# Attention followed by soft MoE: q loaded one quad earlier, the first quads reordered, the MoE mask moved, three expert weights issued later, and three small edits in the tail

One core of a Trainium2 chip. The metric is the time of one execution on the device, in microseconds; every run is checked against the reference.

## The reference

```python
# q, k, v: (8, 12, 448, 64) float32; phi: (768, 32); w1: (8, 768, 1024); w2: (8, 1024, 768)
q_n, k_n = rmsnorm(q, g_q), rmsnorm(k, g_k)              # over head_dim
attn = softmax(q_n @ k_n.T / 8);  o = attn @ v            # per batch and head
x = o.transpose(0, 2, 1, 3).reshape(3584, 768)
logits = x @ phi                                          # 32 slots, 4 for each of 8 experts
d = softmax(logits, axis=0);  slot_input = d.T @ x
for e in range(8):
    slot_out[e] = relu(slot_input[e] @ w1[e]) @ w2[e]
c = softmax(logits, axis=1);  out = c @ slot_out          # (3584, 768) float32
```

## The kernel before

A quad is four heads of one batch: 24 quads, 3 to a batch. The loop is software-pipelined by hand. In round Q the scores and exponentials of quad Q run, beside the normalisation and transposes of later quads and the output of quad Q - 1; every third round the MoE logits and slot sums of a batch fall in. q, k and v go over the SP queue (448 KB each for a quad); 16 expert weights of 3.1 MB (float32) go over the GpSimd queue, cast to bf16 on the way. The slots meet the experts only when the last batch has been summed, then the output is formed and stored.

```python
place("rawq", 2 * 2 * NT * D, 4)     # four buffers of raw q
place("rawk", 2 * 2 * NT * D, 3)
place("qkn", 2 * NT * 128, 1)        # one buffer of scaled q and one of scaled k
place("vraw", 2 * 2 * NT * D, 2)
...
load(0, 0); load(0, 1)               # (quad, 0 = q / 1 = k), cut: g_q, g_k
load(1, 0); load(1, 1); loadv(0); load(2, 0); load(2, 1); loadv(1)
...
square(1, 1); rowsum(1, 1); rsqrt(2, 1, 2); scaleqk(1, 1); vcopy(0)   # end of the prologue
WQ = [0, 2, 4, 6, 9, 11, 13, 16, 18, 20, 21, 21, 22, NQ, NQ]          # round of each weight's issue
for Q in range(NQ + 2):
    for q4 in (3, 4) if Q == 0 else (Q + 4,):
        if q4 < NQ:
            load(q4, 0); load(q4, 1)
    score(Q, 0)
    if Q + 3 < NQ and Q:
        square(Q + 3, 0)             # ScalarE: the q that was issued in round Q - 1
    if ahead and Q:
        square(Q + 2, 1, True)       # GpSimd: k
    # cut: transposes and evictions of Q + 1, scaleqk(Q + 2, 0), scores 1 to 3, outputs
    if mb is not None:
        moe_logits(mb)               # ends with Exp on ScalarE, then memset(e[0:64, 3], 0) on VectorE
    norm(Q - 1, 1, 1); rowsum(Q + 2, 1)
    # cut: loadv(Q + 3); moe_x; rsqrt(Q + 3); scaleqk(Q + 2, 1)
    moe_evac(Q - 1)
    if mb is not None:
        moe_sin(mb)                  # slot-input matmuls read e
    # cut: scores 5 and 6; loadw(i) where WQ[i] == Q
```

The softmax here doesn't subtract the row's maximum and nothing guards it: scores larger than these inputs give would overflow.

## Time and profile before

| | before |
|---|---|
| median of 3 runs | 293.72 us (290.98 to 295.19) |
| span of the profiled run, clock granted to TensorE | 289.4 us, 0.861 |
| attention ends (last output matmul group starts) | 215.3 us |
| TensorE begins the last group of the expert layers | 252.3 us |
| first output matmul / first output issued | 255.9 / 258.5 us |
| ScalarE's waits for q | 8.2 us, 8 times |

ScalarE squares one q per round, so the starts of these squares date the rounds, and their distances are the length of a round. The profiled run is one of the faster ones of this kernel; about half of its later runs took 292 to 294 us.

### The profile page before, as it was taken

The page shows a single profiled execution, that of the slowest core. Times are in us where ns is not written, and L with a number is a line of the kernel's source. Part 1 is how long each engine was busy: PE and PEld are TensorE (multiplying, and loading weights), DVE is VectorE, ACT ScalarE, POOL GpSimd, SP SyncE. Part 2 cuts the span into 40 slices and gives each one's busy share as a digit, 9 for nine tenths or more (in the row PEclk, how much of TensorE's full clock was granted, in tenths as well). Part 3 has the DMA queues.
Part 4 walks back from the last instruction along what each step waited for, and adds up shares of the span by engine and source line. Part 5 has one row for each costly group of instructions (what it writes and reads, how often), then busy time and mean ns, then how long its engine had stood idle before and what let it go on. Part 6 is the DMA issues. An engine that isn't in the chain of part 4 may idle for free.

```text
span 289.4 us, 8498 instructions
## 1 busy us (share of the span) xinstructions
PE 222.8 (77%) x3564; PEld 159.6 (55%) x3564; DVE 193.3 (67%) x411; ACT 190.5 (66%) x272; POOL 164.1 (57%) x187
## 2 busy tenths in 40 slices
PE   7748888888788888898886889988887764789800
PEld 2326565666565666667654666756666764743300
DVE  5837888798768979888885988887553100158700
ACT  4496999789679988997977899788770000037600
POOL 0466999698867888897884988879302000000000
PEclk9958999999999999999999999999996555555555
DMA  6998999999999899999999999969999999519995
GB/s 187 263 286 218 209 264 246 265 283 228 283 247 271 211 213 241 268 240 279 255 267 260 226 240 243 235 158 195 186 207 211 211 214 210 103 68 408 409 413 228
DMA packets 44918, 69.81 MB, mean 241 GB/s; under 512 B 3920, under 2 KB 36688, under 8 KB 44880
## 3 DMA queue, kind: packets, MB, share of 16 engines
q1 hardware_dynamic: 29184, 44.05, 51.4%
q0 software_dynamic: 15376, 25.22, 48.3%
q8 instruction: 28, 0.46, 0.6%
q14 instruction: 10, 0.08, 0.1%
q10 hardware_dynamic: 320, 0.00, 0.1%
HBM read 83.46 MB, written 11.01 MB: 326 GB/s over the span
## 4 chain that ended last, share of the span: by engine, by line
PE 29%; DVE 20%; DMA 17%; ACT 15%; issue 7%; POOL 6%; SPq 1%; ACTq 0%; POOLq 0%; DVEq 0%
DMA arena<-in_q_dram 14%; ACT arena L246 10%; DVE ss L189 7%; PE sc L245 5%; POOL arena L201 5%; DVE arena L230 5%; PE hTp L461 4%; DVE arena L268 4%; PE soTp L470 4%; PE op L500 4%; PE qkTp L219 3%; PE ov L258 3%; ACT arena L181 2%; DMA arena<-in_k_dram 2%; PE op L501 2%
## 5 line engine op out<-in xcount | busy, mean ns | idle before, releaser
L246 ACT ACTIVATE arena<-sc 128x896 bf16<-128x896 f32 x168 | 143.0, 919 | 7.5 <-PE sc L245 7.4
L245 PE MATMUL sc<-arena 128*128 128x448 bf16 x336 | 92.6, 358 | 21.5 <-ACT arena L246 19.2
L201 POOL TENSOR_TENSOR arena<-arena,rs 128x896 bf16<-128x896 f32 x47 | 80.5, 1714 | 41.0 <-ACT rs L194 35.8
L258 PEld LDWEIGHTS <-arena 128*128 128x128 bf16 x1344 | 57.5, 98 | 18.0 <-issue 0.8
L258 PE MATMUL ov<-arena 128*128 128x65 bf16 (+1 forms) x1344 | 62.9, 198 | 0.2 <-ACT arena L246 0.2
L189 DVE TENSOR_REDUCE ss<-arena 128x14 f32<-128x896 f32 x48 | 51.7, 1077 | 6.1 <-ACT arena L181 6.1
L245 PEld LDWEIGHTS <-arena 128*128 128x128 bf16 x336 | 26.8, 98 | 33.1 <-issue 28.7
L268 DVE TENSOR_TENSOR arena<-ov,rd 128x256 bf16<-128x256 f32 x96 | 40.7, 424 | 3.3
L504 ACT ACTIVATE wown<-op,arena 128x768 f32<-128x768 f32 x14 | 12.4, 900 | 42.3 <-PE op L501 42.3
L179 POOL TENSOR_TENSOR arena<-arena 128x896 f32<-128x896 f32 x21 | 35.4, 1686 | 0.2
L181 ACT ACTIVATE arena<-arena 128x896 f32<-128x896 f32 x27 | 25.6, 950 | 9.8 <-DMA arena<-in_q_dram 8.2
L230 DVE COPY arena<-qkTp 64x896 bf16<-64x896 bf16 x48 | 29.8, 620 | 2.0 <-PE qkTp L219 0.9
L219 PE MATMUL qkTp<-ident,arena 128*128 128x128 bf16 x360 | 27.7, 223 | 2.5 <-DVE arena L226 0.8
L219 PEld LDWEIGHTS <-arena 128*128 128x128 bf16 x360 | 22.9, 100 | 10.1 <-POOL arena L201 5.0
L279 PE MATMUL xTp<-ident,arena 128*128 128x128 bf16 x192 | 18.1, 220 | 11.0 <-DVE arena L268 11.0
L267 DVE RECIPROCAL rd<-ov 128x4 f32<-128x4 f32 x96 | 17.0, 177 | 12.6 <-PE sc L245 6.7
L226 DVE TENSOR_SCALAR arena<-qkTp,gg 128x896 bf16<-128x896 bf16 x24 | 16.4, 684 | 11.8 <-PE qkTp L219 11.0
L279 PEld LDWEIGHTS <-arena 128*128 128x128 bf16 x192 | 12.6, 97 | 18.9 <-DVE arena L268 14.4
L193 ACT ACTIVATE ss<-ss,eps 128x28 f32<-128x28 f32 (+1 forms) x27 | 8.5, 315 | 17.2 <-DVE ss L189 17.2
L282 DVE COPY arena<-xTp 128x1024 bf16<-128x1024 bf16 x24 | 16.4, 683 | 2.1 <-PE xTp L279 2.1
L506 DVE TENSOR_SCALAR wown<-op,arena 128x768 f32<-128x768 f32 x14 | 14.2, 1017 | 4.6 <-PE op L501 4.4
L500 PE MATMUL op<-arena,eT 32*128 32x512 bf16 x28 | 16.0, 616 | 1.4 <-ACT wown L504 0.7
(62 smaller groups left out, 192.7 us busy)
## 6 DMA issues: line engine op xcount, KB each, us to landing
wown<-in_moe_w_dram POOLq DMA_DIRECT2D x11, 1536.0 KB, 15.6
arena<-in_q_dram SPq DMA_DIRECT2D x24, 448.0 KB, 7.6
arena<-in_k_dram SPq DMA_DIRECT2D x24, 448.0 KB, 8.9
out_dram<-wown SPq DMA_DIRECT2D x12, 768.0 KB, 9.0
arena<-in_moe_w_dram POOLq DMA_DIRECT2D x5, 1536.0 KB, 21.3
arena<-in_v_dram SPq DMA_DIRECT2D x48, 128.0 KB, 6.8
arena<-in_v_dram SPq DMA_DIRECT2D x48, 96.0 KB, 7.2
out_dram<-wown SPq DMA_DIRECT2D x4, 384.0 KB, 9.1
```

Of the source, the lines that this page charges most:

```text
L179: nc.gpsimd.tensor_tensor(sq(t), r, r, op=MUL)
L181: nc.scalar.activation(out=sq(t), in_=r, func=ACTF.Square)
L189: nc.vector.reduce_sum(sss[n][:, t], sq(t).rearrange("p (r d) -> p r d", d=D), axis=AX)
L201: (eng or nc.gpsimd).tensor_tensor(qkn(Q, t).rearrange("p s (r d) -> p s r d", r=2), raw(Q, t).rearrange("p r (s d) -> p s r d", d=D), rs. ...
L219: nc.tensor.transpose(pts[t][:, i], qkn(Q, t)[:, s], ident)
L230: nc.vector.tensor_copy(kT(Q)[r, :, hh].rearrange("p w (s c) -> p w s c", s=NT), pt[r, :, 1 - hh:8 - hh])
L245: nc.tensor.matmul(sc[:, j, :S], kT(Q)[:, w].rearrange("p h c -> p (h c)")[:, kc:kc + 128], qT(Q)[:, w], start=True, stop=True)
L246: nc.scalar.activation(out=at("attn", i).rearrange("p (h c) -> p h c", h=2), in_=sc[:, :, :S], func=ACTF.Exp, scale=0.125)
L258: nc.tensor.matmul(ovs[half][:, c, o0:o0 + n], attn(i)[:, c0:c0 + 128], mov, start=(i == 7 * w and c == 0), stop=(i == 7 * w + 6), skip_gr ...
L268: nc.vector.tensor_tensor(xq(Q).rearrange("p c (h w d) -> p c h w d", h=2, w=2)[:, 2 * half:2 * half + 2, :, w], o[:, :, :, :D], rd.to_bro ...
L279: nc.tensor.transpose(xps[Q][:, i], xq(Q)[:, i % 4, i // 4 * 128:i // 4 * 128 + 128], ident)
L500: nc.tensor.matmul(op[:, 0], eTtok(j, s), so4[r, :512], start=True, stop=True, tile_position=tp)
```

## The change

The intent: get rid of the rounds in which ScalarE waits for q, start the steady rhythm earlier, keep VectorE from standing behind ScalarE's exponential in the MoE rounds, and shorten the tail. Three entries of the weights' schedule move one quad later as well (7, 12, 14 for 6, 11, 13).

```diff
-    load(1, 0)
-    load(1, 1)
+    for Q in (1, 2):
+        load(Q, 0)
+        load(Q, 1)
     loadv(0)
-    load(2, 0)
-    load(2, 1)
+    load(3, 0)
     loadv(1)
@@ moe_logits / moe_sin
-        nc.vector.memset(e[0:64, 3], 0.0)      # in moe_logits, behind the Exp
     def moe_sin(b):
         e = es.pop(b)
+        nc.vector.memset(e[0:64, 3], 0.0)
@@ prologue
-    scaleqk(0, 1, nc.vector)
+    scaleqk(0, 1)                              # on GpSimd
-    rsqrt(2, 1, 2)
-    scaleqk(1, 1)
+    square(2, 0)
     vcopy(0)
-    WQ = [0, 2, 4, 6, 9, 11, 13, 16, 18, 20, 21, 21, 22, NQ, NQ]
+    WQ = [0, 2, 4, 7, 9, 12, 14, 16, 18, 20, 21, 21, 22, NQ, NQ]
@@ loop
-        for q4 in (3, 4) if Q == 0 else (Q + 4,):
-            if q4 < NQ:
-                load(q4, 0)
-                load(q4, 1)
+        if Q == 0:
+            load(4, 0)
+            load(3, 1)
+        elif Q + 4 < NQ:
+            load(Q + 4, 1)
+            if Q + 5 < NQ:
+                load(Q + 5, 0)
@@ in round 0, ahead of score(Q, 3)
+            rsqrt(2)
+            scaleqk(1, 1)
+            trans(1, 0)
+            evac(1, 0)
+            scaleqk(2, 0)
+            square(3, 0)
+            rowsum(3, 0)
@@ in round 0, the v loads: loadv(2); load(5, 0); load(4, 1); loadv(3)
@@ experts
-        nc.vector.tensor_copy(soT[:, :, e * Spe:(e + 1) * Spe], sp)
+        nc.vector.tensor_copy(soTr.rearrange("p (dc r s) -> p dc r s", dc=DC, r=4)[:, :, :, e * Spe:(e + 1) * Spe],
+                              sp.unsqueeze(2).to_broadcast([128, DC, 4, Spe]))
-    loadw(2 * E - 1)
+    for fc in (0, FC // 2):                    # last weight in two halves; its matmuls run half by half
+        nc.gpsimd.dma_start(out=wt[2 * E - 1][:, fc:fc + FC // 2], in_=wsrc(2 * E - 1)[:, fc:fc + FC // 2])
-    nc.vector.tensor_copy(soTr..., soT.unsqueeze(2).to_broadcast([128, DC, 4, NS]))
@@ output
-            if s % 2 == 1 or s == SO - 1:
-                s0 = s - s % 2
+            if s % 2 == 1 or s == SO - 1 or j + s == 0:      # the first slot goes out alone
+                s0 = s - s % 2 if j + s != 1 else 1
```

The rest of the diff removes what moved from round 0's old places.

More of the change, by code (lines that the diff above doesn't have):

```diff
@@ L350 @@
         if Q == 0:
-            square(2, 0)
             rowsum(2, 0)
-        if Q + 3 < NQ and Q:
-            square(Q + 3, 0)
-        if ahead and Q:
-            square(Q + 2, 1, True)
+        else:
+            if Q + 3 < NQ:
+                square(Q + 3, 0)
+            if ahead:
+                square(Q + 2, 1, True)
         if 0 <= Q - 1 < NQ:
@@ L370 @@
             rowsum(2, 1)
-            rsqrt(2, 0, 1)
         if 0 <= Q - 1 < NQ:
@@ L379 @@
             norm(Q - 1, 1, 0)
-        if Q + 3 < NQ and Q:
+        if Q == 0:
+            rsqrt(2)
[5 more added lines that the diff above has]
+            rowsum(3, 0)
+        elif Q + 3 < NQ:
             rowsum(Q + 3, 0)
@@ L392 @@
             rowsum(Q + 2, 1)
-        for q3 in (2, 3) if Q == 0 else (Q + 3,):
-            if q3 < NQ:
-                loadv(q3)
+        if Q == 0:
+            loadv(2)
+            load(5, 0)
+            load(4, 1)
+            loadv(3)
+        elif Q + 3 < NQ:
+            loadv(Q + 3)
         if on:
@@ L399 @@
         if Q == 0:
-            for t in range(2):
-                trans(1, t)
-                evac(1, t)
-                if t == 0:
-                    scaleqk(2, 0)
-            square(3, 0)
-            rowsum(3, 0)
+            trans(1, 1)
+            evac(1, 1)
         if 0 <= Q - 1 < NQ:
@@ L450 @@
         nc.vector.reciprocal(cinv[:, j:j + 2], cs[:, :, :SO])
-    soT = at("xT", 0)[:, :DC * NS].rearrange("p (dc s) -> p dc s", dc=DC)
     hTs = at("xT", 1)[:, :E * FC * Spe].rearrange("p (e fc s) -> p e fc s", e=E, fc=FC)
@@ L467, in layer2 @@
         sp = psum.tile([128, DC, Spe], F32, tag="misc", name="soTp")
-        for dc in range(DC):
-            for fc in range(FC):
-                nc.tensor.matmul(sp[:, dc], wt[2 * e + 1][:, fc, dc * 128:(dc + 1) * 128],
-                                 hTs[:, e, fc], start=(dc == 0 and fc == 0),
-                                 stop=(fc == FC - 1), skip_group_check=True)
-        nc.vector.tensor_copy(soT[:, :, e * Spe:(e + 1) * Spe], sp)
+        order = [(fc, dc) for dc in range(DC) for fc in range(FC)]
+        for fc, dc in sorted(order) if e == E - 1 else order:
+            nc.tensor.matmul(sp[:, dc], wt[2 * e + 1][:, fc, dc * 128:(dc + 1) * 128],
+                             hTs[:, e, fc], start=(dc == 0 and fc == 0),
+                             stop=(fc == FC - 1), skip_group_check=True)
+        nc.vector.tensor_copy(soTr.rearrange("p (dc r s) -> p dc r s", dc=DC, r=4)[:, :, :, e * Spe:(e + 1) * Spe],
+                              sp.unsqueeze(2).to_broadcast([128, DC, 4, Spe]))
     layer1(0)
-    loadw(2 * E - 1)
+    for fc in (0, FC // 2):
+        nc.gpsimd.dma_start(out=wt[2 * E - 1][:, fc:fc + FC // 2], in_=wsrc(2 * E - 1)[:, fc:fc + FC // 2])
     for e in range(E):
@@ L480 @@
         layer2(e)
-    nc.vector.tensor_copy(soTr.rearrange("p (dc r s) -> p dc r s", dc=DC, r=4),
-                          soT.unsqueeze(2).to_broadcast([128, DC, 4, NS]))
     sop = psum.tile([128, HD], BF16, tag="misc", name="sop")
```

## The prediction

> **What bounds the kernel now.** I read the cores view (span 289.4 us), then the busy rows of the page, the waits, the chain, the timelines of single engines, and the DMA view cut to short windows. The two DMA rows come first: 40 slices of 7.2 us.
>
> ```profile
> DMA  6998999999999899999999999969999999519995
> GB/s 187 263 286 218 209 264 246 265 283 228 283 247 271 211 213 241 268 240 279 255 267 260 226 240 243 235 158 195 186 207 211 211 214 210 103 68 408 409 413 228
> ```
>
> The queues are hardly ever empty until the weights are in (slice 34), and the last slices are the output at some 410 GB/s. Being occupied is not being at the limit, so I took rates from windows with one kind of traffic: q and k alone (18.5 to 21 us), mostly v (22 to 26.5 us), weights alone (225 to 245 us; the bytes are those written in bf16, twice as many are read).
>
> ```profile
> DMA packets 565, 0.95 MB, mean 381 GB/s; under 512 B 34, under 2 KB 565, under 8 KB 565
> DMA packets 1180, 1.02 MB, mean 226 GB/s; under 512 B 134, under 2 KB 1179, under 8 KB 1179
> DMA packets 2450, 4.23 MB, mean 212 GB/s; under 512 B 48, under 2 KB 1500, under 8 KB 2446
> ```
>
> From these, the least DMA time: q and k 22.0 MB / 381 = 57.8 us, v 11.0 MB / 226 = 48.7 us, a weight block 1.573 MB / 212 = 7.4 us. Up to the last v (landing near 194.5 us) the kernel moves q, k, v and nine weight blocks: 57.8 + 48.7 + 9 x 7.4 = 173 us of the 192.5 us since the first packet, 90%. So DMA is no absolute limit in the attention loop, but it has only a tenth to give.
>
> The steady loop has a clean rhythm. I dated each quad by ScalarE's square of q (the timeline of ScalarE): undisturbed, the distances are 7.60, 7.70 and 8.95 us, the long one where the MoE of a batch falls in. In the chain of waits the clean stretch goes around through VectorE, GpSimd and TensorE:
>
> ```profile
> 171.69 0.99 DVE ss L189
> 173.23 1.01 DVE ss L189
> 175.04 1.72 POOL arena L201
> 176.81 0.62 PE qkTp L219 x8
> ...
> 142.34 10.59 DMA arena<-in_q_dram
> 152.95 0.95 ACT arena L181
> ```
>
> The last two lines are the other case: q issued at 142.34 us, its square starting at 152.95 us. The waits view sums it up, and ScalarE's timeline has the worst one:
>
> ```profile
> ACT arena L181 <- DMA arena<-in_q_dram: 8.2, 8, 2.0
> 152.95 0.95 ACT L181 ACTIVATE arena<-arena 128x896 f32<-128x896 f32 x1 [2.00 <-DMA arena<-in_q_dram]
> ```
>
> So the loop is bound by the row sum / rsqrt / scale / transpose circle through VectorE (21.85 us busy of 25.2 in a clean stretch), and is broken by late q. After 216 us come the two expert layers on TensorE, then the output.
>
> **What the Trainium skill says.** "DMA: Bandwidth & Descriptors", Queues, rings and completion order: each DMA engine takes turns between the queues packet by packet, and DMAs of one queue start in order. The trace agrees with the shape: during a weight block q lands late (10.6 us above against a median of 7.6). Its Bandwidth section puts the ceiling at 435 GB/s; the weights read 2 x 212 = 424 GB/s, so the tail's DMA is at its limit. "Runtime: NRT & Kernel Launch", Instruction fetch mechanics: instructions come in blocks of 256, the fetch "mostly hidden". Here it is not: in the expert layers TensorE stands 2.1 to 2.4 us after every 128 load/multiply pairs. "SBUF — State Buffer", SBUF: two separate sides: a VectorE operation with two SBUF inputs and GpSimd lock each other out of a port pair; the change moves the only scaling that VectorE does to GpSimd. No row isolates that lock here.
>
> **Part 1, q five quads ahead.** Before, q(Q+4) is issued at the start of quad Q and its square comes at the start of quad Q+1: one quad of lead, 8 us, against landings of up to 11.8 us. Now it has two quads, 16 us; k and v keep the two they had. The raw q buffers are four and the one reused is read a quad earlier, so no wait is added. The gain: the squares of quads 4 and 23 stand at 27.94 and 186.15 us, 158.2 us for 19 distances. Clean they would be 6 x 8.95 + 13 x 7.65 = 153.2 us. So 5.0 us, not the 8.2 us of the wait, as part of each stop is caught up at the next quad.
>
> **Part 2, the first quads.** GpSimd's timeline shows what the steady circle has to wait for at the start:
>
> ```profile
> 21.92 1.72 POOL L201 TENSOR_TENSOR arena<-arena,rs 128x896 bf16<-128x896 f32 x1 [1.60 <-DMA arena<-in_k_dram]
> 25.72 1.72 POOL L201 TENSOR_TENSOR arena<-arena,rs 128x896 bf16<-128x896 f32 x1 [2.08 <-DMA arena<-in_v_dram]
> 28.41 1.69 POOL L179 TENSOR_TENSOR arena<-arena 128x896 f32<-128x896 f32 x1
> ```
>
> The names of the releasers are doubtful: by program order the first waits for the transposes of k's predecessor in the one buffer, the second for the rsqrt of the third quad. The change has q2 and k2 loaded before v0, so ScalarE can square them before the first exponential. I walked the new order with the old durations. The first key scale moves to GpSimd: 9.65 to 11.4 us, third scale 11.65 to 13.3, v copy about 14 to 15.6 (v0 now lands near 14). The first exponential starts near 13.8 instead of 15.4; rsqrt of the pair ends near 17.6. Then GpSimd: scale 17.6 to 19.3, scale to 21.0, v copy to 22.6, scale 22.6 to 24.3. The old kernel ends that last scale at 27.44, so the circle starts **3.1 us** earlier. The DMA order supplies it: k3 is the eleventh block, about 19 to 20 us, wanted at 25.
>
> **Part 3, the mask.** VectorE's memset waited for ScalarE's exponential of the MoE logits, in front of the norm and the row sum:
>
> ```profile
> 180.80 0.16 DVE L267 RECIPROCAL rd<-ov 128x4 f32<-128x4 f32 x1 [0.41 <-PE sc L245]
> 180.81 0.07 DVE L292 MEMSET e<- 64x16 uint32 x1
> 183.58 0.39 DVE L304 TENSOR_TENSOR sacc<-sinp,sacc 128x224 f32<-128x224 f32 x1 [0.57 <-PE sinp L299]
> ```
>
> The 0.41 us goes, but now the slot-input matmuls wait for the memset behind the xT copy (ends 182.6 instead of 183.0), and VectorE waits for those matmuls next. Worked through, the sum into sacc comes only about 0.1 us earlier. Seven times: **0.8 us**.
>
> **Part 4, the tail.** Three lines of the timeline, and the landing times of the weights' line:
>
> ```profile
> 252.32 1.44 PE L470 MATMUL soTp<-arena,wown 128*128 128x4 bf16 x48
> 254.01 0.36 DVE L483 COPY arena<-arena 128x768 bf16<-128x768 bf16 x1
> 258.47 19.86 SPq L509 DMA_DIRECT2D out_dram<-wown  x16
> DMA to landing us min/median/max: 10.8/16.6/28.2
> ```
>
> The replication copy (0.36 us) goes; each expert's copy writes four times as many elements and grows from 0.18 to about 0.26 us, of which only the last is on the path: 0.3 us. The first output slot goes out alone, one VectorE eviction (1.02 us) less a little queueing earlier; the output runs at 410 GB/s from there to the end, so an earlier start is an earlier end: 0.7 us. The last weight is issued at 224.04 us and lands 28.2 us later, at 252.2, just as TensorE comes to it (252.32). Alone, its two halves gain nothing; if TensorE comes earlier than the weight, they save up to half of the 48 matmuls' 1.28 us. Sum of the tail: **1.0 us**.
>
> **The sum.** Unhindered: 3.1 + 5.0 + 0.8 = 8.9 us up to the end of attention. But the DMA work of 173 us would then have to fit into about 183.5 us, 94% instead of 90%, and the weights' queue, which is busy without a gap from 195 us to the end, sets when the last weight is there. That last point I judge, not compute: I take off a third and keep 6.0 us. With the tail, 7.0 us: 293.7 - 7.0 = **286.7 us**.
>
> **The rivals.** (1) DMA is the real bound: late q is only the symptom, and once q is early, k or v is late instead, or the last weight. For it: 90% occupancy, and the weight stream of 58 us behind quad 20 that ends together with TensorE's work. Against it: k and v have two quads of lead and hardly any wait in the loop; the rates of the single streams were reached only in stretches. Then only 2 to 3 us come, near 290.5 us. (2) The circle through VectorE was never waiting as long as the sums say, or GpSimd (22.1 us of 25.2 in the clean stretch) becomes the bound, since it gets one more scaling at the start: the front gains 1 us, the loop 3, some 288.5 us. (3) Everything fits: 8.9 + 1.0 give 283.8 us; for it speaks that two quads of lead cover the longest landing, 11.8 us, with 4 us to spare. (4) The front goes wrong, because v0 comes after q2 and k2 and GpSimd's v copy holds up the scales behind it: the 3 us become a loss of 1, near 290 us.
>
> **Range and chances.** The old runs spread from 290.98 to 295.19 us, so the ratio alone carries about half a per cent. Rivals 1 and 4 give the upper end, 291, rival 3 with a little luck the lower, 282.5. The 2% line lies at 287.8 us, 1.1 us above my number; most of the range lies below it: faster 0.62, same 0.36, slower 0.02, as nothing added is long enough to cost 6 us.
>
> **What would show it.** Right: ScalarE's wait for q gone from the loop (under 1 us of 8.2), squares at distances of 7.6, 7.7 and 8.9 us throughout; the last scale of the first quad ending near 24.3 us and the fourth quad's square near 24.8; the memset no longer ahead of the norm, the stop before the sum into sacc grown from 0.57 to about 0.9 us; the copy at L483 gone; first output issued one eviction earlier. Rival 1 shows as waits of GpSimd on k or v, or of TensorE on the last weight with TensorE standing before it by more than the 2.4 us of a fetch. The prediction is wrong if the squares keep distances over 8.3 us on average with no wait for q, or if attention ends 9 us earlier and the expert layers end less than 5 us earlier.

## The result, and the profile after

Faster. Ratios here are the mean time of one kernel's fast runs over the mean of the other's fast runs of the same rounds, so not quite the ratio of the medians.

| | before | after |
|---|---|---|
| first result: median | 293.81 us (4 runs) | 282.89 us (4 runs), ratio 0.9624 [0.9542, 0.9705] |
| second, five rounds | 292.84 us | 284.16 us, ratio 0.9703 [0.9646, 0.9759] |
| third, five rounds | 292.06 us | 283.42 us, ratio 0.9704 [0.9644, 0.9764] |
| span profiled, clock | 289.4 us, 0.861 | 282.1 us, 0.865 |

One of the four runs of the changed kernel in the first result, 289.46 us, was slow and is not in the ratio. The two long measurements agree on 0.970, about 8.7 us; the first one, with fewer runs, lay at the edge of their intervals. I hold the partial kernels against 0.970. The first four of them ran on a chip without the changed kernel, so they meet it only through the kernel before.

The DMA row of the page after, in tenths for each of 40 slices. It is as full as before: the change moved data earlier, it did not make less of it.

```profile
DMA  6999999999999999999999999989999999629995
```

**q.** The waits view, and ScalarE's timeline with its two stops in the loop (the third of the three is at the very start). The stop at 70 us on GpSimd, for v, belongs to the same spell; GpSimd stands for v once more at 183.84 us, for 1.61 us.

```profile
ACT arena L181 <- DMA arena<-in_q_dram: 5.7, 3, 2.7
75.21 0.95 ACT L181 ACTIVATE arena<-arena 128x896 f32<-128x896 f32 x1 [2.66 <-DMA arena<-in_q_dram]
115.98 0.95 ACT L181 ACTIVATE arena<-arena 128x896 f32<-128x896 f32 x1 [1.00 <-DMA arena<-in_q_dram]
70.21 0.51 POOL L209 CAST arena<-arena 128x384 bf16<-128x384 f32 x1 [2.17 <-DMA arena<-in_v_dram]
```

So the wait is not gone; and q and k now take longer to land (by the page, q alone 12.1 us in the median, 7.6 before). The view of the q and k issues has, before and then after, from issue to landing:

```profile
DMA to landing us min/median/max: 3.2/8.4/11.8
```
```profile
DMA to landing us min/median/max: 3.3/11.3/14.9
```

**The first quads.** GpSimd's timeline: the last scale of the first round and the first square of k, which in the kernel before stood at 25.72 and 28.41 us.

```profile
23.04 1.71 POOL L201 TENSOR_TENSOR arena<-arena,rs 128x896 bf16<-128x896 f32 x1
25.73 1.69 POOL L179 TENSOR_TENSOR arena<-arena 128x896 f32<-128x896 f32 x1
```

**The mask.** VectorE's timeline in a clean MoE round: the memset follows the copy of xT, VectorE then stands 0.88 us for the slot-input matmuls (0.57 before), and the 0.41 us stop in front of the norm is gone. Distances of the squares in such rounds: 8.80 us against 8.95.

```profile
103.13 0.68 DVE L282 COPY arena<-xTp 128x1024 bf16<-128x1024 bf16 x1
103.75 0.07 DVE L295 MEMSET e<- 64x16 uint32 x1
104.70 0.39 DVE L304 TENSOR_TENSOR sacc<-sinp,sacc 128x224 f32<-128x224 f32 x1 [0.88 <-PE sinp L299]
```

**The tail.** The timeline after:

```profile
244.99 1.05 PE L478 MATMUL soTp<-arena 128*128 128x4 bf16 x34 [1.75 <-issue]
245.90 1.42 PE L478 MATMUL soTp<-arena,wown 128*128 128x4 bf16 x48
247.35 0.26 DVE L481 CAST arena<-soTp 128x96 bf16<-128x96 f32 x1 [1.02 <-PE soTp L478]
247.67 0.56 PEld L495 LDWEIGHTS <-arena 128*128 128x128 bf16 x6 [0.44 <-DVE arena L481]
250.90 6.87 SPq L517 DMA_DIRECT2D out_dram<-wown  x7
```

From the end of the last expert's matmuls to the transposes it is now 0.35 us (245.90 + 1.42 to 247.67) instead of 0.67 us; from the first output matmul to the first store 1.76 us instead of 2.57.

Where the 7.3 us between the two profiled runs lie, by the squares (quad 5 is squared at 35.58 us before and 32.90 after, quad 23 at 186.15 and 179.99) and the marks of the table:

| stretch | before | after | gain |
|---|---|---|---|
| start to the square of quad 5 | 35.58 | 32.90 | 2.68 |
| square of quad 5 to square of quad 23 | 150.57 | 147.09 | 3.48 |
| to the last group of attention's output matmuls | 29.16 | 28.25 | 0.91 |
| to the first output matmul | 40.59 | 40.90 | -0.31 |
| to the end | 33.48 | 32.92 | 0.56 |

### The profile page after: what moved, and what is told of

Same layout as the page of the kernel before. It is cut to its first block, busy times and chain, and to the rows that moved or that the text cites. A ratio compares the mean times of both kernels' runs of the same rounds, so it can differ in the third digit from the quotient of the medians.

```text
span 282.1 us, 8500 instructions
## 1 busy us (share of the span) xinstructions
PE 220.8 (78%) x3564; PEld 158.6 (56%) x3564; DVE 192.2 (68%) x409; ACT 189.6 (67%) x270; POOL 166.6 (59%) x189
## 4 chain that ended last, share of the span: by engine, by line
PE 25%; DVE 22%; DMA 17%; ACT 16%; issue 7%; POOL 7%; ACTq 0%; POOLq 0%
DMA arena<-in_q_dram 17%; ACT arena L246 11%; DVE ss L189 8%; POOL arena L201 7%; DVE arena L230 5%; DVE arena L268 4%; PE hTp L468 4%; PE op L508 4%; PE soTp L478 4%; PE qkTp L219 3%; PE sc L245 3%; ACT arena L181 2%; PE op L509 2%; PE sinp L299 2%; PE ov L258 1%
## 5 line engine op out<-in xcount | busy, mean ns | idle before, releaser
L201 POOL TENSOR_TENSOR arena<-arena,rs 128x896 bf16<-128x896 f32 x48 | 82.2, 1713 | 26.8 <-ACT rs L194 24.7
L512 ACT ACTIVATE wown<-op,arena 128x768 f32<-128x768 f32 x14 | 12.4, 899 | 42.6 <-PE op L509 42.6
## 6 DMA issues: line engine op xcount, KB each, us to landing
arena<-in_q_dram SPq DMA_DIRECT2D x24, 448.0 KB, 12.1
arena<-in_k_dram SPq DMA_DIRECT2D x24, 448.0 KB, 10.9
```

Of the source, the lines that this page charges most:

```text
L201: (eng or nc.gpsimd).tensor_tensor(qkn(Q, t).rearrange("p s (r d) -> p s r d", r=2), raw(Q, t).rearrange("p r (s d) -> p s r d", d=D), rs. ...
```

## The experiments

Twelve runs on top of the two profiles: one part alone, one part left out, and the weights taken out of the loop. My theory then was that DMA is what the loop still waits for; the rivals are named with each.

### q alone

Edit to the kernel before; all else as it was:

```diff
+        elif Q + 4 < NQ:
+            load(Q + 4, 1)
+            if Q + 5 < NQ:
+                load(Q + 5, 0)         # and load(5, 0) between loadv(2) and loadv(3) in round 0
```

> The kernel before with only q loaded five quads ahead. Theory A (the prediction's step one with nothing taken off: DMA has room): ScalarE's wait for q leaves the loop but for a stray microsecond or two, and the time falls by 5 us or somewhat more, to a ratio of 0.98 or below against the kernel before. Theory B (the third that the prediction took off: DMA is the bound, lateness moves to k, v or to the last weight): 2 to 3 us, ratio 0.990 or above, with new waits of GpSimd on k or v.

Measured: median 288.43 us, ratio 0.9869 [0.9805, 0.9932]: 3.8 us (1.3% of 293), between the two expectations. In its profile q is waited for twice, once at the start and once (0.88 us) in the loop.

The squares of quads 4 and 23 are 154.34 us apart, 3.9 us less than before (158.21). So in the loop nearly everything that was to be had came.

### q left out

The changed kernel with load(Q + 4, 0) and load(Q + 4, 1) again in round Q, and no load(5, 0) in round 0.

> The changed kernel with q back at four quads ahead, all else kept. Theory A (parts add up): it loses 5 us or somewhat more against the changed kernel (0.9624 of before), so a ratio of 0.98 or above; the q waits of before (about 8 us in the whole profile) come back. Theory B (the earlier start already uses up the DMA's reserve, so q ahead is worth little on top): it loses 2 us at most, ratio under 0.970.

Measured: median 289.1 us, ratio 0.9887 [0.9841, 0.9934]. Against 0.970 that is 0.018 or 5.4 us lost. The waits are back, and are longer than in the kernel before:

```profile
ACT arena L181 <- DMA arena<-in_q_dram: 11.3, 8, 2.3
```

Theory B falls: with the other parts in place, q ahead is worth 5.4 us, not 2 at most. Whether that is more than the 3.8 us that it gave alone, the intervals do not say. The other parts without it gain 3.3 us together (1.1% of 293).

### The first quads left out

> The changed kernel with the first quads in the old order, all else kept. Theory A: loses the 3 us that the start of the steady circle gained (the square of k in quad 1 on GpSimd back from 25.7 to about 28.4 us), ratio about 0.972. Theory B (DMA-bound loop gives the early start back): ratio within 0.003 of the changed kernel's 0.9624, since the loop would only wait for data longer.

The kernel: the old order of loads, scales and squares in the prologue and in round 0, with q five ahead from round 1 on, the mask, the new weight rounds and the tail of the change.

Measured: median 284.42 us, ratio 0.9736 [0.9693, 0.9779], 1.0 us worse than 0.970, which the intervals do not resolve. In the profile the early rounds are back where they were (GpSimd's first square of k at 28.50 us, against 25.73), but the square of quad 23 is at 181.09 us, only 1.1 us behind the changed kernel's 179.99. On the way the changed kernel stood 2.66 us for q at 75 us and 1.00 us at 115 us; this one stood once, 1.37 us. Of the 2.7 us won at the start the loop of this profile gave back more than half. In the time Theory B is nearer; the profiles do not decide, for in two other executions of the changed loop (the changed kernel again, and the old tail, both below) the square of quad 23 came at 178.62 and 178.40 us, 2.5 and 2.7 us ahead of this kernel's.

### The mask left out, and the mask alone

> The changed kernel with the MoE mask back behind the exponential, all else kept. Theory A (the prediction): the clean distance of the squares where a batch's MoE falls in goes from 8.8 back to 8.95 us, 7 times, so about 1 us, ratio about 0.966. Rival: more than that (2 us or more, ratio 0.969 or above), because VectorE's stop for the mask was up to 1.5 us long in the kernel before, not 0.41.

Measured: median 284.95 us, ratio 0.9755 [0.9703, 0.9808], 1.5 us worse than 0.970; the intervals overlap. The profile is clearer: MoE rounds are 8.95 us apart instead of 8.80, and from the square of quad 23 to the last output group it takes 29.16 us instead of 28.25. In the profiles of the changed kernel, of the one without the first quads and of the mask alone this last stretch is 28.25 us; with the mask in its old place (before, and the change without the mask) it is 29.16 us, with q ahead alone 29.17. The one exception among the fast profiles with the weights in the loop is the second one of the changed kernel (31.36 us), where v was late; see below. So the mask takes 6 x 0.15 + 0.91 = 1.8 us off the circle, half of it in one round.

The chain of waits shows what happens in that round (22, the first without row sums, where VectorE is free and TensorE leads). Before:

```profile
203.63 0.59 PE lg L288 x24
204.22 0.40 PE sc L245 x2
204.62 0.19 issue
204.81 0.17 DVE rd L267
204.98 0.02 issue
205.00 0.43 DVE arena L268
205.44 0.05 issue
205.49 0.51 PE xTp L279 x6
```

After:

```profile
197.47 0.59 PE lg L288 x24
198.07 0.39 PE sc L245 x2
198.45 0.45 PE xTp L279 x8
```

Before, TensorE had to wait for VectorE's reciprocal and norm, which stood behind the mask, which stood behind ScalarE's exponential. After, the norm has long been done.

Then the mask alone, in the kernel before:

```diff
-        nc.vector.memset(e[0:64, 3], 0.0)      # in moe_logits
     def moe_sin(b):
         e = es.pop(b)
+        nc.vector.memset(e[0:64, 3], 0.0)
```

> The kernel before with only the mask moved. Theory A (clean stretches alone: 6 x 0.15 us in the loop and 0.9 us at quad 22, as the profiles of the changed kernel with and without the mask show): 1.8 us, ratio about 0.994. Rival (the mask also passes ScalarE's lateness on to VectorE, so where q is late it costs more): 3 us or more, ratio 0.990 or below. The prediction's 0.8 us: ratio 0.997.

Measured: median 292.94 us, ratio 1.0009 [0.9954, 1.0065]: nothing, and both the 1.8 us and the rival's 3 us are outside or at the edge of the interval. Its profile has the shorter last stretch (28.25 us), but its waits for q have grown from 8.2 to 10.9 us:

```profile
ACT arena L181 <- DMA arena<-in_q_dram: 10.9, 7, 2.2
```

A shorter round with the same lead in rounds is a shorter lead in microseconds: as long as q comes one round ahead, what the mask saves may be waited off on q. That is argued, not shown: it is one profile each, and the one of the kernel before is of one of its fastest runs. In the expert layers TensorE's last stop (see the tail below) is also longer here, 2.30 us against 0.93, which is more than the last stretch had saved.

### The changed kernel again, and the old tail

> The changed kernel itself once more, on one chip with the runs beside it, as the base that the partial kernels are held against. All theories: ratio 0.9624 again within its interval, 0.954 to 0.971.

Measured: ratio 0.9703, as in the table above.

Its profile (fast, span 283.3 us) shows how far one execution can be read. The square of quad 23 comes at 178.62 us, 1.4 us earlier than in the first profile, and the waits for q sum to 4.8 us. But then GpSimd stands 3.1 us for a v that was issued at 172.52 us and landed 12.4 us later; the chain of waits goes through it, and from that square to the last output group it takes 31.36 us instead of 28.25.

```profile
185.06 0.51 POOL L209 CAST arena<-arena 128x384 bf16<-128x384 f32 x1 [3.10 <-DMA arena<-in_v_dram]
```

So two fast profiles of one kernel differ by 1 to 3 us in a stretch, and some of the lateness has moved from q to v, as the prediction's first rival said it would.

The old tail is the kernel before from the first line behind the loop on:

> The changed kernel with everything after the attention loop as before (replication by one copy, last weight in one piece, output in pairs from the first slot on). Theory A (the prediction): 1.0 us slower than the changed kernel, ratio up by 0.003 to 0.004. Rival (the two halves of the last weight matter, since TensorE now stands before it): 1.6 us or more, ratio up by 0.0055 or more, and TensorE waiting before the last expert's second layer.

Measured: median 283.24 us, ratio 0.9685 [0.9636, 0.9733], the same as the changed kernel's 0.9703. So the tail's edits cannot be told from nothing in the time, and the rival is refuted by the profile: TensorE shows no wait for the last weight before its last group. The profiles show why there is little to see. The pieces are there (0.32 us from the copy; 0.56 us from first output matmul to the end), but the run with the old tail happened to leave attention 1.6 us earlier (206.64 against 208.24 us), and something in the expert layers gave part of it back: from the last output group to the first output matmul it took 41.67 us against 40.90.

What gives it back can be read. In the expert layers TensorE stands after every 128 load/multiply pairs. The last such stop, in the timelines of two kernels:

```profile
251.41 1.04 PE L470 MATMUL soTp<-arena 128*128 128x4 bf16 x34 [0.93 <-issue]
```
```profile
243.06 1.05 PE L478 MATMUL soTp<-arena 128*128 128x4 bf16 x34 [2.57 <-issue]
```

The first is the kernel before, the second the last experiment below, with three weights later. With the old tail the stop is 2.30 us, with the change 1.75. It is short where the weights' stream has nearly run out when TensorE gets there (in the kernel before, the DMA engines are busy 23% of the last microsecond ahead of it), and about as long as the other stops where it has not (93% in the last experiment). So an earlier end of attention is not wholly an earlier output: up to 1.6 us (2.57 - 0.93) of it goes into this stop. That the stop is an instruction fetch that queues behind the weights is argued from the regular 128 pairs, not shown by a run that changes it.

### The weights' rounds as before

```diff
-    WQ = [0, 2, 4, 7, 9, 12, 14, 16, 18, 20, 21, 21, 22, NQ, NQ]
+    WQ = [0, 2, 4, 6, 9, 11, 13, 16, 18, 20, 21, 21, 22, NQ, NQ]
```

> The changed kernel with the old quads for the weights' issue (three of them one quad earlier). Theory A (the new quads were chosen because DMA is tight): the same or up to 2 us slower, with a q wait at another quad. Rival (the 2 us wait for q near 75 us, which all kernels with the new quads show and q_only with the old ones does not, comes from the new quads): that wait goes and the time falls by 1 to 2 us.

Measured: median 285.81 us, ratio 0.9797 [0.9736, 0.9857] against 0.9703 [0.9646, 0.9759]: 0.0094, some 2.7 us, the intervals just touching. The fast runs of the two differ by 2.5 us in the mean, with a standard error of 0.8: that the old rounds cost time is shown, how much only roughly. Theory A is nearer, with a loss at or over its upper end, and the rival falls: the wait near 75 us shrinks to 1.21 us but a longer one comes at 149 us,

```profile
149.03 0.95 ACT L181 ACTIVATE arena<-arena 128x896 f32<-128x896 f32 x1 [4.05 <-DMA arena<-in_q_dram]
```

and the sum of the waits for q is 9.0 us. By these numbers the smallest edit of the diff is worth more than the first quads, the mask or the tail, though the intervals overlap. The profile is of this kernel's fastest run (span 282.9 us, less than the 283.3 of the changed kernel's beside it), so it shows where q is late and not the whole loss. With the old rounds but without the early first quads, q ahead alone stood only 0.88 us for q in its loop: what the weights' rounds are worth depends on the other parts, and moving them in the kernel before was not tried.

### The weights out of the loop

Both kernels with every weight issued after the last quad's loop body, to see the loop without their traffic. The results are right; the totals, 361.63 and 355.43 us, are of no interest.

```diff
+    WQ = [NQ - 1] * 10 + [NQ - 1, NQ - 1, NQ - 1, NQ, NQ]
```

> The kernel before with every weight issued after the last quad's loop body; the result is right, the total is much longer (thirteen weights of 7.4 us one after another), and only the attention loop is looked at. Theory A (the weights' share of the DMA engines makes q late): no wait for q in the loop, squares of quads 4 to 23 about 153 us apart instead of 158.2. Rival (the one quad of lead is too short anyway): waits of 0.5 us or more stay, and over 155 us.

Measured: the squares of quads 4 and 23 are 153.37 us apart, with distances of 7.6, 7.7 and 8.95 us (one pair of 7.80 and 7.55) and no wait for q in the loop; the one left is at the start. Attention's last output group starts at 209.71 us instead of 215.31.

```profile
ACT arena L181 <- DMA arena<-in_q_dram: 2.1, 1, 2.1
arena<-in_q_dram SPq DMA_DIRECT2D x24, 448.0 KB, 4.2
```

The second line is of the page's DMA issues: q lands 4.2 us after its issue, against 7.6 us with the weights beside it. So one round of lead is enough in itself; it is the weights that make it too short.

> The changed kernel with every weight issued after the last quad's loop body; only the attention loop is looked at. Theory A (DMA is what is left to wait for in the changed loop): no wait for q, k or v in the loop, clean distances 7.6, 7.7 and 8.8 us throughout, so 6 x 8.8 + 12 x 7.65 = 144.6 us from the fifth square to the last against 147.1 and 145.8 us measured; GpSimd, freed of the weights' issues (0.9 us each), may add a little. Rival (the engines' circle is the limit already): the same distances as with the weights.

Measured: 144.75 us from the square of quad 5 to that of quad 23 (147.09 in the changed kernel), all distances 7.6, 7.7 or 8.79 us, no wait of ScalarE for q after round 0 (there, 0.57 us at 17.75 us). The waits view does name v for 11.1 us of GpSimd's idle time, in 6 pieces; since the distances are clean, it is idle time that cost nothing, and whether v was really its releaser I leave open. Attention's last output group starts at 204.52 us.

### Three early weights one round later still

The remaining stop at 75 us is in the first third of the loop, where the quads now start 3 us earlier with the same data behind them. So I moved three early weights:

```diff
-    WQ = [0, 2, 4, 7, 9, 12, 14, 16, 18, 20, 21, 21, 22, NQ, NQ]
+    WQ = [0, 3, 5, 7, 10, 12, 14, 16, 18, 20, 21, 21, 22, NQ, NQ]
```

> The changed kernel with three of the early weights one quad later (0, 3, 5, 7, 10 in place of 0, 2, 4, 7, 9). Theory A (DMA is behind in the first third of the loop, since the quads now start 3 us earlier with the same data to fetch): the q wait of about 2 us near 75 us goes or shrinks below 1 us and the time falls by 1 to 2 us, ratio 0.003 to 0.006 below the base. Rival (the wait only moves to a later quad, total DMA work being what it is): the same time within 0.003.

and, as the base,

> The changed kernel once more as the base of this call. Ratio to the kernel before between 0.962 and 0.976, as its two earlier values with their intervals say.

Measured: median 281.85 us, ratio 0.9681 [0.9622, 0.974], against 283.42 us and 0.9704 [0.9644, 0.9764]. In the time the difference, 0.0023, is inside the noise. In its profile ScalarE waits for q only at the start; the second line is the landing of q and k:

```profile
ACT arena L181 <- DMA arena<-in_q_dram: 2.1, 1, 2.1
DMA to landing us min/median/max: 3.3/9.1/14.9
```

The distance from the square of quad 5 to that of quad 23 is 144.75 us, to the hundredth what the loop takes without any weight in it, while DMA moves 260 GB/s in that stretch (254 in the changed kernel). So it is not the amount of data that made q late here, but where the weights fall. Attention's last output group starts at 205.59 us, 2.65 us before the profiled changed kernel's, and the span is 280.0 us, 2.1 us less; part of the rest went into the stop of 2.57 us shown above. With its clean loop I would keep this version, but that it is faster than the change is not shown by the times.

## Why the prediction was right, and where it was not

It said 286.7 us, faster by 7.0 us. The profiled runs differ by 7.3 us; the timed runs by about 8.7 us, the first ones by 11. By its steps:

- **What bounds the loop.** Right. A circle of 7.6, 7.7 and 8.95 us through VectorE and GpSimd, broken by late q: the loop without weights has just these distances, 153.4 us where the prediction computed 153.2.
- **q, 5.0 us.** Right in mechanism, and near in size: 3.8 us alone, 5.4 us when left out. The expectation that the wait falls below 1 us failed: 3.7 us stayed in the profiled loop (2.66 and 1.00). q's lead doubled, but q's landing grew from a median of 7.6 to 12.1 us (q and k together from 8.4 to 11.3, at most 14.9); that this is because more is queued at a time is argued.
- **The first quads, 3.1 us.** Right where it was worked out (2.7 us: the last scale ends at 24.75 us where 24.3 was said, the first square of k 2.7 us earlier). As a share of the total it was too much: 1.0 us when left out, which the intervals do not tell from nothing. The walk ended where the circle begins, and the prediction carried its whole gain to the end of attention; but the changed kernel's profiles all stand for q near 75 us (2.66, and 1.75 in the second), and with three early weights a round later that stop is gone.
- **The mask, 0.8 us.** The mis-sized term: 1.8 us in the profiles. The 0.15 us per clean round is the 0.1 that was said; what failed is "Seven times". The seventh MoE round of the loop is round 22, where no row sums stand beside it and VectorE's stop lies on the path of TensorE: 0.91 us. The profile had a hint, VectorE's stop of 1.33 us in just this round. And alone the mask is worth nothing, so the terms of the sum were not independent.
- **The tail, 1.0 us.** The pieces are there in the profile (0.3 and 0.6 us), the halves of the last weight gain nothing as predicted, and the stop of TensorE that grew from 0.93 to 1.75 us gives most of it back. The prediction had seen these stops ("2.1 to 2.4 us"), but not that the last one was short and could grow. In the time there is nothing to see.
- **"I take off a third".** A judgement, and in the profiled pair about right: 2.7 + 3.5 + 0.9 = 7.1 us came up to the end of attention where 8.9 was worked out (5.3 us in the second profile). What it stood for, DMA with only a tenth to give, is not what the runs show. Without the weights q is in time, but with as many of them in the loop as before and three early ones a round later still, q is in time too, and attention ends 9.7 us earlier than in the kernel before (205.59 against 215.31 us). What hindered was where the weights fall. That a third was about the right size is luck.
- **The rivals.** Of the first, one sign came: v is late in the changed kernel (2.17 us at 70 us, 3.10 us in the second profile), and TensorE did not stand for the last weight. Its number is slightly off: 2 to 3 us less than 293.7 is 290.7 to 291.7, not near 290.5.
- **What was not in the sum at all:** the three weights' rounds, some 2.5 us. The prediction used the old schedule's spacing only to compute the DMA time, though it called the weights the limit's larger part. That missing term is large enough for the difference of 1.7 us between the timed gain and the prediction, and the third rival ("everything fits", 283.8 us) is close to the measured medians for this reason and not for its own: two quads of lead did not cover the landings, which grew with it, and the moved weights made room.

## What to carry to other kernels

Where a software pipeline shares DMA with a second stream, the lead of a load is measured in rounds: whatever shortens the round shortens the lead, and a saving on the engines shows only after the load has been moved ahead. Before adding lead, run the loop once with the other stream taken out; if the waits vanish, try spreading that stream as well: it costs no buffer, and here it was worth some 2.5 us beside the 3.8 to 5.4 us of the deeper prefetch. And an early start can pay in full only if the data of the rounds that follow is early too; the profiles point to it, the times do not show it.

## What the Trainium skill lacked or had wrong

- "Runtime: NRT & Kernel Launch", Instruction fetch mechanics, calls the cost of crossing an instruction block mostly hidden. In the expert layers TensorE stands 1.6 to 2.6 us after every 128 pairs of a load and a very short matmul, which is such a block, while the weights stream, some 10 us in all (the five stops of the changed kernel sum to 10.7 us), and 0.93 us where the stream has nearly ended. The page does not say that the fetch may be slowed by other DMA; the runs suggest it and do not prove it.
- "DMA: Bandwidth & Descriptors" lists, for trn2, rates by the size of a transfer. Here transfers of 448 KB back to back reach 381 GB/s with q's and k's runs of 1792 bytes, and 226 GB/s in a window that is mostly v, in pieces of 768 and 1024 bytes: no table there gives rates for loads by run length. The runs do not separate it from the rest: the transfers of v are also smaller (96 and 128 KB) and go to 64 partitions each.
- The same page says that the engines take turns between queues, but gives no figure for what that does to a small load beside a large one: q takes 4.2 us from issue to landing without the weights and 7.6 us with them, and 12.1 us once q is queued a round deeper.
